# Turning the output in 32x32 squares on VectorE instead of transposing it on TensorE, in a spectral filter followed by a SiLU block

## Chip, cores, metric

One core of one Trainium2 chip. The metric is device time of one execution in microseconds; "before" has a median of 2844.55 us (2841.62 to 2846.77, 4 runs). In the text, TensorE is also PE, VectorE is DVE, ScalarE is ACT, GpSimd is POOL and SyncE is SP, as in the profile.

## The reference

```python
x: (8, 3008, 256) f32; filt_r, filt_i: (1505, 256) f32; w_in: (256, 2048); w_out: (2048, 256)
X = np.fft.rfft(x, axis=1)
y = np.fft.irfft(X * (filt_r + 1j * filt_i)[None], n=3008, axis=1).astype(np.float32)
h = y.reshape(24064, 256) @ w_in
out = (h / (1 + np.exp(-h)) @ w_out).astype(np.float32)
```

## The kernel before

The FFT is done as matmuls in three stages per batch (`spectral`: stage 1, forward, filter multiply, inverse, stage 3). Stage 3 leaves y with channels on the partitions and positions along the free dimension. A "half" of a batch has 16 x 94 = 1504 positions; three "pairs" of chunks cut them. Both products with the weights are done in 2x2 blocks with seven instead of eight block products (the w_t of sums and differences), over 8 steps per pair: in a step, `hidden` makes one slice of the hidden layer in the PSUM tiles px and pyz (one buffer each), and `project` multiplies the previous slice with w_out into `acc`. After the eighth step `drain` copies `acc` to s, seven adds combine it, and `output` transposes and stores. Pieces of the next batch's `spectral` are put between the rounds of these steps.

```python
PAIRS = [(0, 252), (504, 250), (1004, 250)]      # first position, columns of one chunk
CH = 252
...
        def stage3(u):
            g, cb = divmod(u, 2)
            if cb == 0 and g < 7:
                load_t4(g + 1)
            ps = bank(b, f"pd_{b}_{u}").rearrange("p a c -> p (a c)")
            psv = ps[:, 0:4 * NR].rearrange("p (a r) -> p a r", r=NR)      # NR = 94
            for i in range(4):
                nc.tensor.matmul(out=psv[:, i, :], lhsT=t4s[g][:, i, cb * 128:cb * 128 + 128],
                                 rhs=wi_t, start=True, stop=True)
            ...   # 376 columns, cut at the pairs' borders, evicted as they come: order n', row
                    evac(y[pair][:, cb, p0 - c0:p1 - c0], ps[:, p0 - lo:p1 - lo])
...
    def output(pair, chunk):
        b, half, c0, n = pairs[pair]
        s, m = results[pair], n // 2
        ps = fps.tile([128, 2, 2, 128], FP32, name=f"pt_{pair}_{chunk}", tag="f")
        for blk in range(2):
            for h in range(2):
                src = ((2, 6), (4, 1))[chunk][h]
                nc.tensor.transpose(out=ps[0:m, blk, h], in_=s[:, src, m * blk:m * blk + m],
                                    identity=id_t)
        o = opool.tile([128, 2, C], FP32, name=f"o_{pair}_{chunk}", tag="o")
        evac(o[0:m], ps[0:m].rearrange("p k h c -> p k (h c)"))     # DVE and ACT in turn
        for blk in range(2):
            store(o, blk, m, b, half, c0 + n * chunk + m * blk)     # rows of 1 KB, issued by POOL
...
        for g, (step, rnd) in enumerate(((-11, 3), (-7, 3), (-3, 3), (0, 3), (9, 3), (15, 6), (29, 3), (33, 3))):
            put(step, rnd, stage3, 2 * g); put(step, rnd, stage3, 2 * g + 1)
```

Of the kernel before, what the change touches and what calls it, by code (L numbers as in the profile page):

```python
# [49 lines left out]
NJP = NJ // 2  # L53
HALF = 16 * NR

PAIRS = [(0, 252), (504, 250), (1004, 250)]
CH = 252
STEPS = 2 * len(PAIRS) * NJP
LAG = 1

# [77 lines left out]
def kernel(  # L138
# [14 lines left out]
    wi_dram = nc.inline_tensor(wi_host, name="wi_tbl")  # L153
    d_dram = nc.inline_tensor(d_host, name="d_tbl")
    e_dram = nc.inline_tensor(e_host, name="e_tbl")
    id_dram = nc.inline_tensor(np.eye(128, dtype=np.float32), name="id_tbl")

    def pool(name, bufs, space=None):
        kw = {} if space is None else {"space": space}
        return ctx.enter_context(tc.tile_pool(name=name, bufs=bufs, **kw))  # L160

    cpool = pool("consts", 1)
    ypool = pool("y", 4)
    typool = pool("ty", 2)
    xpool = pool("x", 1)
    upool = pool("u", 1)
    t1pool = pool("t1", 2)
    t2pool = pool("t2", 2)
    ppool = pool("p", 2)
    zpool = pool("z", 3)  # L170
    qpool = pool("q", 2)
# [15 lines left out]
    f_t = [cpool.tile([128, NG, 2, C], FP32, name=f"filt{i}") for i in range(2)]  # L187

    w_t = cpool.tile([128, 7, 2, NJP, 128], FP32)
    id_t = cpool.tile([128, 128], FP32)  # L190
    warm = cpool.tile([128, 1], FP32)
    x_t = [xpool.tile([128, 2, 2, C], FP32, name=f"x{i}") for i in range(2)]

# [34 lines left out]
    def spectral(b):  # L228
# [7 lines left out]
        def load_x(u):  # L236

            if b == 0 and u < 4:
                xs[u] = ypool.tile([128, 2, 512], FP32, name=f"x_{b}_{u}", tag="y")
                nc.gpsimd.memset(xs[u][32:64], 0.0)  # L240
            else:
                xs[u] = x_t[u % 2]
            for h in range(2):
                for r0, nr in ((0, 32), (32, N1 - 32)):
                    nc.sync.dma_start(
                        out=xs[u][64 * h + r0:64 * h + r0 + nr],
                        in_=bass.AP(tensor=x.tensor,
                                    offset=x.offset + (b * S + 32 * r0 + 4 * u + 2 * h) * C,
                                    ap=[[32 * C, nr], [32 * N1 * C, 2], [1, 2 * C]]))
# [9 lines left out]

        def stage1(u):  # L260
            ut = us.pop(u)
            t1 = t1pool.tile([128, 2, 2, C], FP32, name=f"t1_{b}_{u}", tag="t1")
            ps = [bank(b, f"pa_{b}_{u}_{h}") for h in range(2)]
            for par in range(2):
                for h in range(2):
                    rows = slice(64 * h, 64 * h + N1)
                    nc.tensor.matmul(out=ps[h][64 * par:64 * par + 64], lhsT=wf_t[rows, par],  # L267
                                     rhs=ut[rows, par], start=True, stop=True)
            for h in range(2):
                evac(t1[:, h], ps[h])  # L270
            for par in range(2):
                nc.gpsimd.dma_start(  # L272
                    out=d1[par].rearrange("s p n c -> (s p) n c")[:, 4 * u:4 * u + 4, :],
                    in_=t1[64 * par:64 * par + 2 * NS].rearrange("p h n c -> p (h n) c"))

        def load_t2(g):
            t2s[g] = t2pool.tile([128, 4, C], FP32, name=f"t2_{b}_{g}", tag="t2")
            for par in range(2):
                nc.sync.dma_start(out=t2s[g][64 * par:64 * par + 64],
                                  in_=d1[par, 4 * g:4 * g + 4].rearrange("s p n c -> (p n) s c"))  # L280
# [52 lines left out]
        def stage3(u):  # L333
            g, cb = divmod(u, 2)
            half = g // 4
# [3 lines that stand above are left out]
            psv = ps[:, 0:4 * NR].rearrange("p (a r) -> p a r", r=NR)  # L339
            for i in range(4):  # L340
                nc.tensor.matmul(out=psv[:, i, :], lhsT=t4s[g][:, i, cb * 128:cb * 128 + 128],  # L341
                                 rhs=wi_t, start=True, stop=True)

            lo, hi = 4 * NR * (g % 4), 4 * NR * (g % 4 + 1)
            for k, (c0, n) in enumerate(PAIRS):
                p0, p1 = max(lo, c0), min(hi, c0 + 2 * n)
                if p0 < p1:
                    pair = (2 * b + half) * len(PAIRS) + k
                    if pair not in y:
                        y[pair] = ypool.tile([128, 2, 512], FP32, name=f"y_{pair}", tag="y")  # L350
                    evac(y[pair][:, cb, p0 - c0:p1 - c0], ps[:, p0 - lo:p1 - lo])

        at = STEPS * b
        pieces = []
# [15 lines left out]
            put(3 * g - 35, 1, add, g, 1)  # L370
            put(3 * g - 35, 3, inverse, g)
        put(-18, 5, load_t4, 0)
        for g, (step, rnd) in enumerate(((-11, 3), (-7, 3), (-3, 3), (0, 3), (9, 3), (15, 6), (29, 3), (33, 3))):
            put(step, rnd, stage3, 2 * g)
            put(step, rnd, stage3, 2 * g + 1)
        if b > 0:
# [9 lines left out]
    def combine(eng, out, in0, in1, op):  # L386
        eng.tensor_tensor(out=out, in0=in0, in1=in1, op=op)  # L387

    def tokens(pair):

        n, yt = pairs[pair][3], y[pair]
        t = typool.tile([128, 4, CH], FP32, name=f"ty_{pair}", tag="ty")
        combine(v, t[:, 0:2, 0:n], yt[:, :, n:2 * n],
                yt[:, 0, 0:2 * n].rearrange("p (a n) -> p a n", a=2), ALU.subtract)
        combine(v, t[:, 2, 0:n], yt[:, 1, n:2 * n], t[:, 0, 0:n], ALU.subtract)
        combine(v, t[:, 3, 0:n], yt[:, 1, 0:n], t[:, 2, 0:n], ALU.subtract)
        ty[pair] = t

    def hidden(step):

        pair, jp = divmod(step, NJP)
        n, yt, t = pairs[pair][3], y[pair], ty[pair]
        px = xps.tile([128, 512], FP32, name=f"px_{step}", tag="x")
        pyz = xps.tile([128, 2, 256], FP32, name=f"pyz_{step}", tag="yz")
        sums = abcpool.tile([128, 3, CH], FP32, name=f"abc_{step}", tag="abc")
# [70 lines left out]
    def drain(pair, i):  # L476
        n = pairs[pair][3]

        if i == 0:
            results[pair] = spool.tile([128, 8, CH], FP32, name=f"s_{pair}", tag="s")  # L480
        s = results[pair]
        copy = v.tensor_copy if i % 2 else nc.scalar.copy
        if i < 3:
            copy(out=s[:, 2 * i:2 * i + 2, 0:n], in_=acc[pair][i][:, :, 0:n])  # L484
            return
        copy(out=s[:, 6, 0:n], in_=acc.pop(pair)[3][:, 0, 0:n])
        eng = v if pair == len(pairs) - 1 else gp
        for o, a, b in ((2, 0, 2), (5, 0, 5), (3, 5, 3), (6, 3, 6), (0, 5, 1), (4, 0, 4), (1, 3, 1)):
            combine(eng, s[:, o, 0:n], s[:, a, 0:n], s[:, b, 0:n], ALU.add)

    def output(pair, chunk):

        b, half, c0, n = pairs[pair]
        s, m = results[pair], n // 2
        ps = fps.tile([128, 2, 2, 128], FP32, name=f"pt_{pair}_{chunk}", tag="f")
        for blk in range(2):
            for h in range(2):
                src = ((2, 6), (4, 1))[chunk][h]
                nc.tensor.transpose(out=ps[0:m, blk, h], in_=s[:, src, m * blk:m * blk + m],  # L499
                                    identity=id_t)  # L500
        o = opool.tile([128, 2, C], FP32, name=f"o_{pair}_{chunk}", tag="o")
        evac(o[0:m], ps[0:m].rearrange("p k h c -> p k (h c)"))
        for blk in range(2):
            store(o, blk, m, b, half, c0 + n * chunk + m * blk)

    def store(o, blk, m, b, half, col):
        p = 0
        while p < m:
            n, r = divmod(col + p, NR)
            cnt = min(m - p, NR - r)  # L510
            t0 = b * S + 32 * r + 16 * half + n
            nc.gpsimd.dma_start(  # L512
                out=bass.AP(tensor=out.tensor, offset=out.offset + t0 * C, ap=[[32 * C, cnt], [1, C]]),
                in_=o[p:p + cnt, blk, :])
            p += cnt

    wide = moe_w_in.dtype != FP32
    nc.vector.memset(warm, 0.0)
# [7 lines left out]
    def places(j, w):  # L526
        first, by = PLACES[j % 2][w]
        return w_t[:, first:first + by + 1:by, w, j // 2]

    def load_weights(j):  # L530

# [7 lines left out]
    def round_weights(j):  # L539
# [15 lines left out]
        v.scalar_tensor_tensor(out=mf, in0=lo, scalar=2.0 ** -52, in1=mf, op0=ALU.mult, op1=ALU.add)  # L555
        for w in range(2):
            cols = slice(256 * w, 256 * w + 256)
            gp.tensor_tensor(out=places(j, w), in0=mf[:, cols].rearrange("p (k n) -> p k n", k=2),
                             in1=ef[:, cols].rearrange("p (k n) -> p k n", k=2), op=ALU.mult)
        if j % 2:  # L560
            combine_weights(j // 2)
        if j + 2 < NJ:
# [2 lines left out]
    def load_exact(j):  # L565
        for k in range(2):
            nc.sync.dma_start(out=places(j, 0)[:, k],
                              in_=moe_w_in[128 * k:128 * k + 128, 128 * j:128 * j + 128])
            nc.sync.dma_start(out=places(j, 1)[:, k],
                              in_=moe_w_out[128 * j:128 * j + 128, 128 * k:128 * k + 128])  # L570
        if j % 2:
            combine_weights(j // 2)

# [8 lines left out]
    def constants():  # L582
# [1 line left out]
        load_filters()  # L584
        nc.scalar.dma_start(out=e_t, in_=e_dram.ap())
        nc.scalar.dma_start(out=wi_t, in_=wi_dram.ap())
        nc.scalar.dma_start(out=id_t, in_=id_dram.ap())

    nc.sync.dma_start(out=wf_t, in_=wf_dram.ap())
    for xt in x_t:  # L590
# [15 lines left out]
        pending += [(-39 + 1.9 * j, NJ, lambda j=j: load_exact(j)) for j in range(NJ)]  # L606
    per = len(PAIRS) * 2

    stores = ((10, 3), (18, 6), (30, 3), (35, 3), (43, 3), (51, 6))
    for pair in range(len(pairs)):  # L610
        pending.append((NJP * pair - 2 + (5 if pair % per == 3 else 1) / ROUNDS, 100,
                        lambda pair=pair: tokens(pair)))
        step, rnd = stores[pair % per]
        for chunk in range(2):
            pending.append((pair // per * STEPS + step + rnd / ROUNDS, 99 + chunk,
                            lambda pair=pair, chunk=chunk: output(pair, chunk)))
    pending.sort(key=lambda p: p[:2])
# [49 lines left out]
```

## Time and profile before

| | before |
|---|---|
| span of the profiled run | 2842.5 us |
| PE / DVE / ACT / POOL busy | 2713 / 1627 / 1103 / 726 us |
| one batch in mid-kernel | 336.27 us, PE idle 1.5 us of it |
| the 8 transposes of a pair, in PE's stream | 0.88 us |
| transposes' evictions | 96, of 0.69 us (DVE) or 0.59 us (ACT) |
| stores | 432, issued by POOL, 0.53 us each |

"Busy" is time in which an engine has an instruction in flight. PE's instructions overlap, so their summed durations exceed their cost; the cost of a PE group is read from the starts in the timeline. PEld is TensorE loading the weights of a matmul; an "eviction" is the copy of a finished PSUM tile to SBUF by DVE or ACT; the "granted clock" is the share of full speed that TensorE was given. In the timeline, a row has start, length, engine, line, operation, out<-in, shape and count; what stands in brackets is the engine's idle time just before and what ended it.

### The profile page before, as it was taken

What the parts mean: (1) busy time and instruction counts of PE and PEld (TensorE: products, weight loads), DVE (VectorE), ACT (ScalarE), POOL (GpSimd) and SP (SyncE); (2) the same over time, 40 slices, a digit from 0 to 9 for tenths busy, and PEclk for the clock granted to TensorE, in tenths of its full rate; (3) what the DMA queues carried; (4) which work ended last, traced back from release to release, by engine and by line L of the source; (5) the groups of instructions that cost most, each with busy time, mean ns of one, the idle gap of its engine ahead of it and who ended that gap; (6) DMA issues with size and microseconds to landing.
All of it is one profiled execution on the core that took longest, in us unless ns stands there. A gap on an engine that the chain in (4) does not pass through costs nothing.

```text
span 2842.5 us, 39974 instructions
## 1 busy us (share of the span) xinstructions
PE 2713.2 (95%) x14976; PEld 2292.8 (81%) x14976; DVE 1627.1 (57%) x3416; ACT 1103.0 (39%) x3058; POOL 725.9 (26%) x1155
## 2 busy tenths in 40 slices
PE   2479999999999999999999999999999999999998
PEld 0258889788897888888898888978888788988887
DVE  2876654666556665566655665465655666544554
ACT  0124334443444334443344443444344433444443
POOL 1532222222213312222222232223221321221222
PEclk9779999999999999999999999999999999999999
DMA  8543211232113211232112321123111321000000
GB/s 177 157 120 84 60 34 37 80 74 51 34 35 105 60 42 31 52 98 64 36 36 70 84 50 34 43 79 77 43 39 33 105 63 42 27 28 18 14 15 15
DMA packets 92276, 166.66 MB, mean 59 GB/s; under 512 B 20641, under 2 KB 51441, under 8 KB 91825
## 3 DMA queue, kind: packets, MB, share of 16 engines
q1 hardware_dynamic: 56080, 83.46, 11.2%
q0 software_dynamic: 33536, 75.03, 10.2%
q10 hardware_dynamic: 2464, 5.61, 1.1%
q8 instruction: 118, 1.93, 0.3%
q14 instruction: 78, 0.63, 0.1%
HBM read 89.03 MB, written 74.97 MB: 58 GB/s over the span
## 4 chain that ended last, share of the span: by engine, by line
PE 92%; DVE 4%; DMA 2%; issue 1%; POOL 1%; ACT 0%; SPq 0%; DVEq 0%; ACTq 0%; POOLq 0%
PE acc L468 39%; PE px L412 23%; PE pyz L412 17%; PE pd L341 4%; PE pc L319 3%; PE pa L267 2%; PE pb L290 2%; PE pt L499 1%; DMA filt<-in_filt_r_dram 1%; DVE z L310 0%; DMA d<-t 0%; DVE u L255 0%; DVE g L387 0%; DVE z L309 0%; DMA t<-d 0%
## 5 line engine op out<-in xcount | busy, mean ns | idle before, releaser
L468 PE MATMUL acc<-g,w_t 128*128 128x250 f32 (+1 forms) x5376 | 1512.1, 375 | 0.4 <-DVE g L387 0.4
L468 PEld LDWEIGHTS acc<-g,w_t 128*128 128x128 f32 x5376 | 1021.1, 190 | 116.0 <-DVE g L387 0.8
L387 DVE TENSOR_TENSOR g<-pyz,abc 128x250 f32<-128x250 f32 (+1 forms) x1152 | 480.2, 417 | 641.9 <-ACT abc L433 363.2
L387 DVE TENSOR_TENSOR g<-g 128x250 f32<-128x250 f32 (+3 forms) x1152 | 611.7, 531 | 197.1 <-ACT g L416 183.7
L412 PE MATMUL px<-ty,w_t 128*128 128x250 f32 (+1 forms) x2304 | 692.9, 382 | 0.5 <-ACT abc L433 0.5
L416 ACT ACTIVATE g<-g 128x250 f32<-128x250 f32 (+1 forms) x1152 | 474.0, 411 | 241.2 <-DVE g L387 241.2
L412 PEld LDWEIGHTS px<-ty,w_t 128*128 128x128 f32 x2304 | 415.1, 190 | 123.0 <-issue 71.6
L412 PE MATMUL pyz<-y,w_t 128*128 128x250 f32 (+1 forms) x1536 | 452.8, 376 | 8.8 <-DVE g L387 8.8
L387 POOL TENSOR_TENSOR s<-s 128x250 f32<-128x250 f32 (+1 forms) x329 | 266.4, 826 | 678.3 <-DVE s L484 428.8
L512 POOL DMA_DIRECT2D out_dram<-o x432 | 223.7, 526 | 502.5 <-DVE o L211 495.0
L412 PEld LDWEIGHTS pyz<-y,w_t 128*128 128x128 f32 x1536 | 282.7, 189 | 52.5 <-DVE g L387 15.4
L427 ACT COPY abc<-px 128x250 f32<-128x250 f32 (+1 forms) x384 | 141.7, 369 | 379.7 <-PE px L412 379.7
L416 ACT ACTIVATE g<-px 128x250 f32<-128x250 f32 (+1 forms) x384 | 146.4, 381 | 298.4 <-PE px L412 298.4
L326 POOL DMA_DIRECT2D d<-q x192 | 113.8, 601 | 555.7 <-DVE q L211 553.0
L433 ACT COPY abc<-px 128x250 f32<-128x250 f32 (+1 forms) x384 | 142.0, 370 | 228.0 <-PE px L412 228.0
L412 PE MATMUL pyz<-ty,w_t 128*128 128x250 f32 (+1 forms) x768 | 225.8, 376 | 0.0
L412 PE MATMUL px<-y,w_t 128*128 128x250 f32 (+1 forms) x768 | 225.2, 375 | 0.0
L412 PEld LDWEIGHTS pyz<-ty,w_t 128*128 128x128 f32 x768 | 145.5, 190 | 17.6 <-DVE g L387 1.4
L412 PEld LDWEIGHTS px<-y,w_t 128*128 128x128 f32 x768 | 143.5, 189 | 19.2 <-issue 0.4
L272 POOL DMA_DIRECT2D d<-t x128 | 65.9, 519 | 344.3 <-ACT abc L433 275.9
L341 PEld LDWEIGHTS pd<-wi_t,t 96*128 96x128 f32 x1024 | 129.3, 199 | 20.6 <-issue 11.7
L341 PE MATMUL pd<-wi_t,t 96*128 96x94 f32 x1024 | 128.1, 280 | 17.0 <-issue 11.0
(46 smaller groups left out, 1504.2 us busy)
## 6 DMA issues: line engine op xcount, KB each, us to landing
d<-t POOLq DMA_DIRECT2D x128, 192.0 KB, 3.0
t<-d SPq DMA_DIRECT2D x96, 256.0 KB, 4.0
d<-q POOLq DMA_DIRECT2D x192, 128.0 KB, 2.7
t<-d SPq DMA_DIRECT2D x64, 384.0 KB, 3.8
x<-in_x_dram SPq DMA_DIRECT2D x128, 128.0 KB, 3.1
x<-in_x_dram SPq DMA_DIRECT2D x128, 60.0 KB, 2.9
out_dram<-o POOLq DMA_DIRECT2D x80, 94.0 KB, 2.0
raw<-in_moe_w_in_dram SPq DMA_DIRECT2D x16, 256.0 KB, 2.8
```

The costliest lines, as they stand in the source:

```text
L267: nc.tensor.matmul(out=ps[h][64 * par:64 * par + 64], lhsT=wf_t[rows, par], rhs=ut[rows, par], start=True, stop=True)
L272: nc.gpsimd.dma_start(out=d1[par].rearrange("s p n c -> (s p) n c")[:, 4 * u:4 * u + 4, :], in_=t1[64 * par:64 * par + 2 * NS].rearrange(" ...
L319: nc.tensor.matmul(out=ps[i][:, k, :], lhsT=e_t[rows, g, k, ri, :], rhs=zs[k][rows, ri, :], start=(ri == 0), stop=(ri == 1))
L326: nc.gpsimd.dma_start(out=d2[a0:a0 + 2, :, :].rearrange("s n c -> n s c"), in_=qt[64 * p:64 * p + 64, :, :])
L341: nc.tensor.matmul(out=psv[:, i, :], lhsT=t4s[g][:, i, cb * 128:cb * 128 + 128], rhs=wi_t, start=True, stop=True)
L387: eng.tensor_tensor(out=out, in0=in0, in1=in1, op=op)
L412: nc.tensor.matmul(out=out, lhsT=w_t[:, c, 0, jp], rhs=rhs, start=start, stop=True, skip_group_check=True)
L416: nc.scalar.activation(out=g[:, k, 0:n], in_=g[:, k, 0:n] if src is None else src, func=AFT.Silu)
L427: nc.scalar.copy(out=sums[:, 1, 0:n], in_=xo)
L433: nc.scalar.copy(out=sums[:, 2, 0:n], in_=xo)
L468: nc.tensor.matmul(out=acc[pair][i][:, h, 0:n], lhsT=w_t[:, c, 1, jp], rhs=g[:, k, 0:n], start=(jp == 0 and h == 0), stop=last, skip_group ...
L512: nc.gpsimd.dma_start(out=bass.AP(tensor=out.tensor, offset=out.offset + t0 * C, ap=[[32 * C, cnt], [1, C]]), in_=o[p:p + cnt, blk, :])
```

## The change

The intent is to take the transposes off TensorE. VectorE can transpose 32x32 squares from SBUF to SBUF. For squares to become runs of the output, w_out's columns are permuted as they are loaded, and the tokens are taken in the order row, n' (so y is now one tile for a whole half and stage 3 must be complete before a half's first tokens). Stores go to SP, in runs of 256 bytes. Chunks are multiples of 16.

```diff
-PAIRS = [(0, 252), (504, 250), (1004, 250)]
-CH = 252
+PAIRS = [(0, 256), (512, 256), (1024, 240)]
+CH = 256
...
-            lo, hi = 4 * NR * (g % 4), 4 * NR * (g % 4 + 1)
-            ... (evictions cut at the pairs' borders)
+            if cb == 0 and g % 4 == 0:
+                y[b, half] = ypool.tile([128, 2, HALF], FP32, name=f"y_{b}_{half}", tag="y")
+            evac(y[b, half][:, cb].rearrange("p (r n) -> p n r", n=16)[:, 4 * (g % 4):4 * (g % 4) + 4],
+                 psv)
...
-        for g, (step, rnd) in enumerate(((-11, 3), (-7, 3), (-3, 3), (0, 3), (9, 3), (15, 6), (29, 3), (33, 3))):
+        for g, (step, rnd) in enumerate(((-16, 3), (-12, 3), (-8, 3), (-4, 3), (9, 3), (12, 6), (15, 6), (18, 6))):
...
     def output(pair, chunk):
-        ... (four nc.tensor.transpose, one evac, stores issued by POOL)
+        o = opool.tile([128, 8, 2, 32], FP32, name=f"o_{pair}_{chunk}", tag="o")
+        for h in range(2):
+            v.transpose(out=o[:, :, h, :], in_=results[pair][:, ((2, 6), (4, 1))[chunk][h], :])
+        row = (c0 + n * chunk) // 16
+        for rr in range(2):
+            cnt = (n // 16 - rr + 1) // 2
+            t0 = b * S + 32 * (row + rr) + 16 * half
+            for q in range(4):
+                p0 = 32 * q + 16 * rr
+                nc.sync.dma_start(out=bass.AP(..., ap=[[C, 16], [64 * C, cnt], [1, 64]]),
+                    in_=o[p0:p0 + 16, 0:cnt].rearrange("p k h c -> p k (h c)"))
... (also: permuted loading of w_out, t1 and t2 in one pool of two buffers, y pool of two halves,
     a memset of the unused columns of s, other steps for the outputs, no identity table)
```

More of the change, by code (lines that the diff above doesn't have):

```diff
@@ L155 @@
     e_dram = nc.inline_tensor(e_host, name="e_tbl")
-    id_dram = nc.inline_tensor(np.eye(128, dtype=np.float32), name="id_tbl")
     def pool(name, bufs, space=None):
@@ L162 @@
     cpool = pool("consts", 1)
-    ypool = pool("y", 4)
+    ypool = pool("y", 2)
     typool = pool("ty", 2)
@@ L166 @@
     upool = pool("u", 1)
-    t1pool = pool("t1", 2)
-    t2pool = pool("t2", 2)
+    tpool = pool("t12", 2)
     ppool = pool("p", 2)
@@ L189 @@
     w_t = cpool.tile([128, 7, 2, NJP, 128], FP32)
-    id_t = cpool.tile([128, 128], FP32)
     warm = cpool.tile([128, 1], FP32)
@@ L238, in load_x @@
             if b == 0 and u < 4:
-                xs[u] = ypool.tile([128, 2, 512], FP32, name=f"x_{b}_{u}", tag="y")
+                if u % 2 == 0:
+                    xs[u, "y"] = ypool.tile([128, 2, HALF], FP32, name=f"x_{b}_{u}", tag="y")
+                xs[u] = xs[u - u % 2, "y"][:, u % 2, 0:1024].rearrange("p (a n) -> p a n", a=2)
                 nc.gpsimd.memset(xs[u][32:64], 0.0)
@@ L261, in stage1 @@
             ut = us.pop(u)
-            t1 = t1pool.tile([128, 2, 2, C], FP32, name=f"t1_{b}_{u}", tag="t1")
+            t1 = tpool.tile([128, 2, 2, C], FP32, name=f"t1_{b}_{u}", tag="t")
             ps = [bank(b, f"pa_{b}_{u}_{h}") for h in range(2)]
@@ L276, in load_t2 @@
         def load_t2(g):
-            t2s[g] = t2pool.tile([128, 4, C], FP32, name=f"t2_{b}_{g}", tag="t2")
+            t2s[g] = tpool.tile([128, 4, C], FP32, name=f"t2_{b}_{g}", tag="t")
             for par in range(2):
@@ L342, in stage3 @@
                                  rhs=wi_t, start=True, stop=True)
-            lo, hi = 4 * NR * (g % 4), 4 * NR * (g % 4 + 1)
-            for k, (c0, n) in enumerate(PAIRS):
-                p0, p1 = max(lo, c0), min(hi, c0 + 2 * n)
-                if p0 < p1:
-                    pair = (2 * b + half) * len(PAIRS) + k
-                    if pair not in y:
-                        y[pair] = ypool.tile([128, 2, 512], FP32, name=f"y_{pair}", tag="y")
-                    evac(y[pair][:, cb, p0 - c0:p1 - c0], ps[:, p0 - lo:p1 - lo])
+            if cb == 0 and g % 4 == 0:
+                y[b, half] = ypool.tile([128, 2, HALF], FP32, name=f"y_{b}_{half}", tag="y")
+            evac(y[b, half][:, cb].rearrange("p (r n) -> p n r", n=16)[:, 4 * (g % 4):4 * (g % 4) + 4],
+                 psv)
         at = STEPS * b
@@ L387, in combine, with channels @@
         eng.tensor_tensor(out=out, in0=in0, in1=in1, op=op)
+    def channels(pair):
+        b, half, c0, n = pairs[pair]
+        return y[b, half][:, :, c0:c0 + 2 * n]
     def tokens(pair):
-        n, yt = pairs[pair][3], y[pair]
+        n, yt = pairs[pair][3], channels(pair)
         t = typool.tile([128, 4, CH], FP32, name=f"ty_{pair}", tag="ty")
@@ L401, in hidden @@
         pair, jp = divmod(step, NJP)
-        n, yt, t = pairs[pair][3], y[pair], ty[pair]
+        n, yt, t = pairs[pair][3], channels(pair), ty[pair]
         px = xps.tile([128, 512], FP32, name=f"px_{step}", tag="x")
@@ L480, in drain @@
             results[pair] = spool.tile([128, 8, CH], FP32, name=f"s_{pair}", tag="s")
+            if n < CH:
+                gp.memset(results[pair][:, :, n:CH], 0.0)
         s = results[pair]
@@ L493, in output @@
         b, half, c0, n = pairs[pair]
-        s, m = results[pair], n // 2
-        ps = fps.tile([128, 2, 2, 128], FP32, name=f"pt_{pair}_{chunk}", tag="f")
-        for blk in range(2):
-            for h in range(2):
-                src = ((2, 6), (4, 1))[chunk][h]
-                nc.tensor.transpose(out=ps[0:m, blk, h], in_=s[:, src, m * blk:m * blk + m],
-                                    identity=id_t)
-        o = opool.tile([128, 2, C], FP32, name=f"o_{pair}_{chunk}", tag="o")
-        evac(o[0:m], ps[0:m].rearrange("p k h c -> p k (h c)"))
-        for blk in range(2):
-            store(o, blk, m, b, half, c0 + n * chunk + m * blk)
-    def store(o, blk, m, b, half, col):
-        p = 0
-        while p < m:
-            n, r = divmod(col + p, NR)
-            cnt = min(m - p, NR - r)
-            t0 = b * S + 32 * r + 16 * half + n
-            nc.gpsimd.dma_start(
-                out=bass.AP(tensor=out.tensor, offset=out.offset + t0 * C, ap=[[32 * C, cnt], [1, C]]),
-                in_=o[p:p + cnt, blk, :])
-            p += cnt
+        o = opool.tile([128, 8, 2, 32], FP32, name=f"o_{pair}_{chunk}", tag="o")
[7 more added lines that the diff above has]
+                p0 = 32 * q + 16 * rr
+                nc.sync.dma_start(
+                    out=bass.AP(tensor=out.tensor, offset=out.offset + t0 * C + 64 * q,
+                                ap=[[C, 16], [64 * C, cnt], [1, 64]]),
+                    in_=o[p0:p0 + 16, 0:cnt].rearrange("p k h c -> p k (h c)"))
     wide = moe_w_in.dtype != FP32
@@ L528, in places, with columns @@
         return w_t[:, first:first + by + 1:by, w, j // 2]
+    def columns(ap, w):
+        if w == 0:
+            return ap.rearrange("p (k n) -> p k n", k=2)
+        return ap.rearrange("p (q k i) -> p k q i", q=4, k=2)
     def load_weights(j):
@@ L557, in round_weights @@
             cols = slice(256 * w, 256 * w + 256)
-            gp.tensor_tensor(out=places(j, w), in0=mf[:, cols].rearrange("p (k n) -> p k n", k=2),
-                             in1=ef[:, cols].rearrange("p (k n) -> p k n", k=2), op=ALU.mult)
+            dst = places(j, w) if w == 0 else places(j, w).rearrange("p k (q i) -> p k q i", q=4)
+            gp.tensor_tensor(out=dst, in0=columns(mf[:, cols], w), in1=columns(ef[:, cols], w),
+                             op=ALU.mult)
         if j % 2:
@@ L568, in load_exact @@
                               in_=moe_w_in[128 * k:128 * k + 128, 128 * j:128 * j + 128])
-            nc.sync.dma_start(out=places(j, 1)[:, k],
-                              in_=moe_w_out[128 * j:128 * j + 128, 128 * k:128 * k + 128])
+            nc.sync.dma_start(out=places(j, 1)[:, k].rearrange("p (q i) -> p q i", q=4),
+                              in_=columns(moe_w_out[128 * j:128 * j + 128, :], 1)[:, k])
         if j % 2:
@@ L586, in constants @@
         nc.scalar.dma_start(out=wi_t, in_=wi_dram.ap())
-        nc.scalar.dma_start(out=id_t, in_=id_dram.ap())
     nc.sync.dma_start(out=wf_t, in_=wf_dram.ap())
@@ L607 @@
     per = len(PAIRS) * 2
-    stores = ((10, 3), (18, 6), (30, 3), (35, 3), (43, 3), (51, 6))
+    stores = (((10, 1), (10, 5)), ((19, 5), (20, 1)), ((28, 5), (29, 1)), ((34, 1), (34, 5)),
+              ((42, 1), (42, 5)), ((50, 1), (51, 1)))
     for pair in range(len(pairs)):
@@ L612 @@
                         lambda pair=pair: tokens(pair)))
-        step, rnd = stores[pair % per]
         for chunk in range(2):
+            step, rnd = stores[pair % per][chunk]
             pending.append((pair // per * STEPS + step + rnd / ROUNDS, 99 + chunk,
```

## The prediction

> **What bounds the kernel now.** I read the page first (engine shares, the rows by slice, the chain that ended last), then the busy time by stretch, the waits, the groups by shape and the timeline. The page of the kernel before:
>
> ```profile
> span 2842.5 us, 39974 instructions
> PE 2713.2 (95%) x14976; PEld 2292.8 (81%) x14976; DVE 1627.1 (57%) x3416; ACT 1103.0 (39%) x3058; POOL 725.9 (26%) x1155
> ...
> PE   2479999999999999999999999999999999999998
> ...
> PE 92%; DVE 4%; DMA 2%; issue 1%; POOL 1%; ACT 0%; SPq 0%; DVEq 0%; ACTq 0%; POOLq 0%
> ```
>
> TensorE is busy in nine tenths of every slice but the first three and the last, and 92% of the chain is its work. "Busy" alone proves little, since matmuls overlap, so I took one whole period in mid-kernel from the view of busy time by stretch:
>
> ```profile
> 1190.47:1526.74 336.27, 334.72 (x1874) 284.37 (x1873) 195.72 (x415) 136.40 (x382) 84.58 (x136) 1.00 0.22 57
> ```
>
> One batch takes 336.27 us; PE is idle 1.55 us of it, at a granted clock of 1.00. DVE (195.72) and ACT (136.40) have large gaps, and the DMA engines are 22% busy. PE's waits over the whole run confirm it: the sizeable ones belong to the start, and the one steady wait is small.
>
> ```profile
> PE pa L267 <- DVE u L255: 48.0, 8, 28.6
> ...
> PE pc L319 <- DVE z L309: 33.6, 7, 7.7
> ...
> PE pyz L412 <- DVE g L387: 8.8, 13, 0.9
> ```
>
> So in the steady stage the time is the sum of what PE streams: a matmul removed is time saved, and one removed from another engine is worth nothing by itself.
>
> **What the Trainium skill says.** (1) "TensorE: Matmul & The Clock Gate", Part 4: a PE transpose takes any 128x128 in one shot, but lands in PSUM and needs a copy after it; about 275 ns in a kernel. The trace agrees (273 ns and a copy of 586 or 692 ns), yet 273 ns is a duration, not the price: the timeline shows what it costs in the stream. (2) "VectorE: DVE Perf Modes", The three transpose paths: VectorE transposes 32x32 blocks only, into SBUF, 311 ns for 128x128 bf16. No transpose on DVE is in this trace; I price it below from this trace's copies. (3) "DMA: Bandwidth & Descriptors", Specifications: line rate needs transfers of at least 512 B. The new runs of 256 B fall below; the trace doesn't yet show such stores. (4) "SBUF — State Buffer", the note on 16-byte cachelines: accesses that change line each time pay. The new evictions into y step 64 B; the ones before are contiguous, so the trace is silent on it.
>
> **The change, part by part.**
>
> PE, removed. Each of 48 pairs had 8 transposes. Around them the stream looks so:
>
> ```profile
> 1260.98 0.58 PE L468 MATMUL acc<-g,w_t 128*128 128x250 f32 x2
> 1261.40 1.04 PE L499 MATMUL pt<-id_t,s 128*126 128x128 f32 x8
> 1262.28 0.59 PE L412 MATMUL px<-ty,w_t 128*128 128x250 f32 x2
> ```
>
> From 1261.40 to the next start at 1262.28 is 0.88 us, so 0.11 us each; the other pairs that I looked at have 0.87 to 0.88 too. 47 pairs lie inside the stream: 47 x 0.88 = 41.4 us. (The chain's 1.4% for this line, 40 us, says the same. The 50 us of summed durations overstates it.)
>
> PE, resized. A product is recorded as two MATMULs; two start 0.42 us apart at 250 columns (1260.98 to 1261.40), 0.211 us each. With 0.110 us for 128 columns the slope is 0.101 / 122 = 0.83 ns a column, with a floor of some 4 ns. Before, a half has 252 + 250 + 250 = 752 columns; after, 256 + 256 + 240 = 752. The number of matmuls stays, so the sum stays: 0 us. At 240 columns a matmul needs about 0.203 us, still over the 0.190 us of a weight load, so no new limit. Forward, inverse and stage 3 matmuls are the same.
>
> DVE and ACT. Out go 96 evictions of the transposes, half on DVE (0.69 us) and half on ACT (0.59):
>
> ```profile
> L499 PE MATMUL pt<-id_t,s 128*125 128x128 f32 x256 | 33.9, 274 | 2.0 <-DVE s L387 2.0
> L211 DVE COPY o<-pt 125x512 f32<-125x512 f32 x32 | 22.1, 690 | 17.0 <-PE pt L499 16.3
> L213 ACT COPY o<-pt 125x512 f32<-125x512 f32 x32 | 18.8, 586 | 36.2 <-PE pt L499 36.2
> L486 DVE COPY s<-acc 128x250 f32<-128x250 f32 x32 | 13.2, 413 | 4.1 <-PE acc L468 4.0
> ```
>
> In come 48 x 2 x 2 = 192 DVE transposes of 128x256. DVE copies take 413 ns at 250 columns and about 691 at 512: 1.06 ns a column, so an estimated 0.42 us each, 81 us in all. DVE gains 81 - 48 x 0.69 = 48 us, ACT loses 28. The evictions into y fall from 192 to 128 instructions but write with a 64 B step; were each twice as long, DVE's half would gain another 35 us. DVE then stands near 60%: no bound. What can reach PE is latency: an output puts two transposes (0.84 us) and perhaps some semaphore waits into DVE's queue, ahead of the adds that free the single px/pyz buffers. One copy of 0.69 us does the same today, and PE's steady DVE waits total 8.8 us. There will be 96 such places instead of 48; I charge 3 us.
>
> POOL and DMA. 432 issues by POOL (223.7 us) go; its seven adds after each drain stay, at 0.83 us each. 768 stores move to SP, whose issues take 0.31 to 0.60 us in this trace: an estimated 350 us, spread over the run. The output's packets grow from 24,064 of 1 KB to 96,256 of 256 B. In the trace 376 B packets take 22 ns and 1 KB ones of the store queue 49; even at 50 ns for each short one the addition is 96,256 x 50 / 16 = 0.30 ms per engine less 0.07 ms, some 8% of the span on engines now about 23% busy. Hidden.
>
> The start. Now all four stage 3 groups of a half must be done before its first tokens, as these are ordered by row. For batch 0 the fourth moves ahead of the first step (it ran at 180.04 us, after the first products at 176.34). DVE is the busy one there (72 of the 87 us from 100 to 187), rounding weights, and that work stays. The added chain is one load of about 4 us, partly under the last roundings, against 1.8 us of PE work that no longer falls inside step 0. I charge +1 us, give or take 4.
>
> The end. After the last product DVE drains and adds, then come transposes, a copy and 9 POOL issues:
>
> ```profile
> 2830.90 2.76 DVE L387 TENSOR_TENSOR s<-s 128x250 f32<-128x250 f32 x7
> ...
> 2833.48 0.83 PE L499 MATMUL pt<-id_t,s 128*125 128x128 f32 x4 [0.28 <-DVE s L387]
> ...
> 2834.55 4.64 POOL L512 DMA_DIRECT2D out_dram<-o x9 [28.57 <-DVE o L211]
> ```
>
> After the change: adds end near 2833.7, the first two transposes 0.84 us later, then 16 issues of SP at about 0.45 us (7.2), then some 2 us to land: 2843.7 against 2842.5, +1 us.
>
> Sum: 2844 - 41.4 + 3 + 1 + 1 = 2807.6; as the three charges are cautious, I say 2806 us, 1.3% less.
>
> **The rivals.** *DVE becomes the wait.* If a transpose took 1 us or more, or the strided evictions doubled and came just before an add that PE needs, each of 96 outputs and 128 evictions could stall PE by some 0.1 to 0.3 us: 10 to 40 us, which eats the gain (2815 to 2845). For it: px and pyz have one buffer each. Against it: DVE is idle 42% of the period, and today's 0.69 us copies leave PE waiting 1.4 us a batch. *SP becomes the wait.* The stores stand in the queue that brings x, t2 and t4, and a store waits there for its transposes; 8 issues are 3.6 us. For it: in-order queue, four times the packets. Against it: loads are issued 1.6 steps or more (over 10 us) ahead and take 3 to 4. If it failed in each batch, +5 us x 8: 2845. *POOL's relief helps.* The adds after a drain no longer queue behind issues and DVE meets fewer port conflicts; but PE waits for neither, so at most a few us (2800). *The prologue moves.* Before 187 us PE loses over 100 us to waits, so a reordering there could give or take 5 to 10 us whatever the transposes do.
>
> **Range and chances.** The 41 us is read from a stream with 0.5% of idle time; the doubts are the start (+-4), the end (+-2) and DVE's latency (0 to 12, one-sided). That gives 2796 to 2819. Faster by over 2% needs 2788, 15 us beyond what PE can give: 0.03. Slower by over 2% needs a new wait of 100 us: 0.02. Within 2%: 0.95.
>
> **What would show it.** Right: no PE transposes, 14,592 matmuls, a batch period of 336.27 - 6 x 0.88 = 331.0 us with PE idle below 3 us, DVE transposes near 0.42 us, DVE near 59%, POOL's busy time down by 220 us. Wrong: PE waits on DVE g or on a t<-d load in mid-kernel, transposes of 0.8 us and more, a first full step later than 187 us, or an end more than 5 us longer after the last product.

## The result, and the profile after

The changed kernel takes 2808.59 us (2807.75 to 2809.27, 4 runs) against 2844.55: a ratio of 0.9874, 95% interval 0.9857 to 0.9891. Here and below, a ratio is the mean time of one kernel's fast runs over that of the other's fast runs of the same rounds, so it is not quite the ratio of the medians quoted.

The page of the changed kernel (its first lines, and the DMA line below the slices):

```profile
span 2806.0 us, 39589 instructions
## 1 busy us (share of the span) xinstructions
PE 2671.0 (95%) x14592; PEld 2255.6 (80%) x14592; DVE 1671.9 (60%) x3528; ACT 1089.1 (39%) x2978; POOL 504.5 (18%) x739
...
DMA packets 184546, 166.56 MB, mean 59 GB/s; under 512 B 121120, under 2 KB 151456, under 8 KB 184096
```

PE has lost 384 instructions, all of them transposes. DVE gained 45 us, POOL lost 221, and short packets went up sixfold. The bound is the same as before. Busy time by stretch, one batch in mid-kernel (columns: stretch, its length, then busy time and count for PE, PEld, DVE, ACT and POOL, granted clock, DMA share, GB/s):

```profile
961.92:1293.16 331.24, 329.70 (x1827) 279.71 (x1826) 201.38 (x429) 134.67 (x370) 56.77 (x84) 1.00 0.24 58
```

A batch takes 331.24 us instead of 336.27: 5.03 us less, with PE idle for the same 1.5 us. The groups by shape, for the operations that are new or altered:

```profile
L497 DVE STREAM_TRANSPOSE o<-s 128x256 f32<-128x256 f32 x192 | 73.7, 422 | 0.3 <-issue 0.3
...
L211 ACT COPY y<-pd 128x376 f32<-128x376 f32 x64 | 51.1, 799 | 123.4 <-PE pd L341 123.4
L209 DVE COPY y<-pd 128x376 f32<-128x376 f32 x64 | 51.0, 797 | 86.1 <-PE pd L341 86.1
```

and the same eviction of 376 columns in the kernel before:

```profile
L211 DVE COPY y<-pd 128x376 f32<-128x376 f32 x32 | 17.6, 550 | 39.1 <-PE pd L341 39.1
...
L213 ACT COPY y<-pd 128x376 f32<-128x376 f32 x32 | 15.1, 472 | 63.7 <-PE pd L341 63.7
```

A VectorE transpose takes 422 ns. The evictions into y, which now write one element every 64 bytes, went from 550 and 472 ns to about 800 on either engine. The waits over the whole run (who waited for whom, total, times, longest; then the same view of SP's own queue):

```profile
PE pyz L411 <- DVE g L382: 8.5, 12, 1.0
```

```profile
SPq L504 <- DVE o L497: 1255.3, 54, 54.6
```

PE's one steady wait for DVE was 8.8 us before and is 8.5 now. SP's queue stands 1255 us at stores, waiting for their transposes; that looks alarming and, as PE's waits show, holds nothing up.

To see where the 36.5 us between the two spans lie, I cut each run at two events of the timeline: the first stage 1 matmuls that fall between products (batch 1's), and the end of the last product. The first rows are of before, the second of after:

```profile
187.74 1.09 PE L267 MATMUL pa<-u,wf_t 47*64 47x512 f32 x8
...
2828.58 1.95 PE L468 MATMUL acc<-g,w_t 128*128 128x250 f32 x8 [0.41 <-DVE g L387]
```

```profile
189.67 1.09 PE L267 MATMUL pa<-u,wf_t 47*64 47x512 f32 x8
...
2790.37 1.89 PE L467 MATMUL acc<-g,w_t 128*128 128x240 f32 x8 [0.41 <-DVE g L382]
```

So the "start" grew from 187.7 to 189.7, the "stream" between the events shrank from 2642.8 to 2602.6, and the "tail" after the last product grew from 12.0 to 13.7: +1.9 - 40.2 + 1.8 = -36.5 us.

### The profile page after: what moved, and what is told of

It is laid out like the page before. It is cut to its first block, busy times and chain, and to the rows that moved or that the text cites. A ratio compares the mean times of both kernels' runs of the same rounds, so it can differ in the third digit from the quotient of the medians.

```text
span 2806.0 us, 39589 instructions
## 1 busy us (share of the span) xinstructions
PE 2671.0 (95%) x14592; PEld 2255.6 (80%) x14592; DVE 1671.9 (60%) x3528; ACT 1089.1 (39%) x2978; POOL 504.5 (18%) x739
## 4 chain that ended last, share of the span: by engine, by line
PE 92%; DVE 4%; DMA 2%; issue 1%; POOL 0%; ACT 0%; SPq 0%; DVEq 0%; ACTq 0%; POOLq 0%
PE acc L467 40%; PE px L411 24%; PE pyz L411 17%; PE pd L341 4%; PE pc L319 3%; PE pa L267 2%; PE pb L290 2%; DVE g L382 1%; DMA x<-in_x_dram 1%; DVE u L255 1%; DVE z L310 0%; DMA d<-t 0%; DVE z L309 0%; DMA t<-d 0%; DMA filt<-in_filt_i_dram 0%
## 5 line engine op out<-in xcount | busy, mean ns | idle before, releaser
L467 PE MATMUL acc<-g,w_t 128*128 128x256 f32 (+1 forms) x5376 | 1512.6, 375 | 0.4 <-DVE g L382 0.4
L382 DVE TENSOR_TENSOR g<-pyz,abc 128x256 f32<-128x256 f32 (+1 forms) x1152 | 479.7, 416 | 614.8 <-ACT abc L432 356.8
L382 DVE TENSOR_TENSOR g<-g 128x256 f32<-128x256 f32 (+3 forms) x1152 | 611.0, 530 | 196.6 <-ACT g L415 183.5
L411 PE MATMUL px<-ty,w_t 128*128 128x256 f32 (+1 forms) x2304 | 694.3, 383 | 0.5 <-ACT abc L432 0.5
L415 ACT ACTIVATE g<-g 128x256 f32<-128x256 f32 (+1 forms) x1152 | 473.0, 411 | 238.4 <-DVE g L382 235.9
L411 PE MATMUL pyz<-y,w_t 128*128 128x256 f32 (+1 forms) x1536 | 454.0, 377 | 8.5 <-DVE g L382 8.5
L382 POOL TENSOR_TENSOR s<-s 128x256 f32<-128x256 f32 (+1 forms) x329 | 265.7, 825 | 1040.4 <-DVE s L485 520.1
L426 ACT COPY abc<-px 128x256 f32<-128x256 f32 (+1 forms) x384 | 141.4, 368 | 381.0 <-PE px L411 381.0
L432 ACT COPY abc<-px 128x256 f32<-128x256 f32 (+1 forms) x384 | 142.7, 372 | 285.0 <-PE px L411 284.8
L411 PE MATMUL pyz<-ty,w_t 128*128 128x256 f32 (+1 forms) x768 | 226.4, 377 | 0.0
L411 PE MATMUL px<-y,w_t 128*128 128x256 f32 (+1 forms) x768 | 225.7, 376 | 0.0
L419 ACT COPY abc<-px 128x256 f32<-128x256 f32 (+1 forms) x384 | 134.1, 349 | 0.1
## 6 DMA issues: line engine op xcount, KB each, us to landing
d<-t POOLq DMA_DIRECT2D x128, 192.0 KB, 3.0
```

The costliest lines, as they stand in the source:

```text
L382: eng.tensor_tensor(out=out, in0=in0, in1=in1, op=op)
L411: nc.tensor.matmul(out=out, lhsT=w_t[:, c, 0, jp], rhs=rhs, start=start, stop=True, skip_group_check=True)
L415: nc.scalar.activation(out=g[:, k, 0:n], in_=g[:, k, 0:n] if src is None else src, func=AFT.Silu)
L419: nc.scalar.copy(out=sums[:, 0, 0:n], in_=xo)
L426: nc.scalar.copy(out=sums[:, 1, 0:n], in_=xo)
L432: nc.scalar.copy(out=sums[:, 2, 0:n], in_=xo)
```

## The experiments

My theory: the gain is the PE time of the transposes and nothing else, less small losses at the start, at the end and in the stream. The rivals: the new chunk sizes, the relief of POOL and of the PSUM buffers, or a cost of the vector work that hides a larger gain. All runs below are right except e5, which is wrong on purpose. Each was timed beside runs of the kernel before (median 2844.1 to 2845.4 us). The start of one and the same prologue varies: over the nine profiles of kernels that share the changed kernel's start (but for its evictions) it lies between 189.1 and 192.7 us. The stream does not vary so: where nothing in it was altered it is 2602.6 or 2602.7 us, four times out of four.

| run | median us | ratio to before | start | stream | tail |
|---|---|---|---|---|---|
| before | 2844.55 | 1 | 187.7 | 2642.8 | 12.0 |
| after | 2808.59 | 0.9874 | 189.7 | 2602.6 | 13.7 |
| e1 sizes alone | 2845.73 | 1.0001 | 188.8 | 2643.3 | 11.9 |
| e2 PE transposes back | 2850.48 | 1.0021 | 189.1 | 2644.7 | 13.7 |
| e3 DVE transposes twice | 2811.65 | 0.9886 | 191.3 | 2604.4 | 14.4 |
| e4 DVE transposes four times | 2895.56 | 1.0180 | 191.7 | 2688.8 | 15.7 |
| e5 plain evictions | 2806.14 | 0.9865 | 190.2 | 2600.6 | 13.7 |
| e6 stores from POOL | 2813.43 | 0.9892 | 192.4 | 2603.2 | 17.4 |
| e7 shorter end | 2805.40 | 0.9864 | 192.7 | 2602.6 | 9.3 |
| e8 earlier loads at the start | 2805.80 | 0.9866 | 188.6 | 2602.7 | 13.7 |
| e9 = e7 + e8 | 2802.51 | 0.9848 | 190.9 | 2602.6 | 9.4 |
| e10 evictions in runs of four | 2806.26 | 0.9862 | 192.0 | 2600.6 | 13.7 |
| e11 the same, by PE's order | 2805.76 | 0.9859 | 189.5 | 2601.1 | 13.7 |
| e12 = e7 + e8 + e11 | 2800.45 | 0.9844 | 189.3 | 2600.7 | 9.4 |

### e1: the sizes alone

```diff
 (kernel before)
-PAIRS = [(0, 252), (504, 250), (1004, 250)]
-CH = 252
+PAIRS = [(0, 256), (512, 256), (1024, 240)]
+CH = 256
```

> The kernel before with pairs of 256, 256 and 240 columns in place of 252, 250 and 250, and nothing else; right results. Theory (TensorE's stream sets the time, 0.83 ns a column plus a floor per matmul): 752 columns a half either way, so the same within 2 us of 2844. Rival (part of the gain comes from sizes that suit the engines better): 10 to 36 us less. If 256 were worse by itself: more than 2850.

Measured: ratio 1.0001 (0.9988 to 1.0013), stream 0.5 us longer. The sizes bring nothing by themselves; they are there because squares of 32 and runs of 16 need them. The sum of columns is the same, and so is the time.

### e2: the TensorE transposes put back

```diff
 (changed kernel, in output)
+        ps = fps.tile([128, 2, 2, 128], FP32, name=f"pt_{pair}_{chunk}", tag="f")
+        for blk in range(2):
+            for h in range(2):
+                nc.tensor.transpose(out=ps[:, blk, h], identity=id_t,
+                                    in_=results[pair][:, ((2, 6), (4, 1))[chunk][h], 128 * blk:128 * blk + 128])
... (also: the identity table and its load)
```

> The changed kernel with the eight TensorE transposes of each pair put back beside the vector engine's, into a PSUM buffer that nobody reads; right results. Theory (the gain is TensorE's removed work, 0.88 us a pair, 48 pairs): 40 to 43 us over the changed kernel, about 2850. Rival (the gain came from the copies, the PSUM buffers or POOL's 432 issues): 0 to 15 us more, under 2825.

Measured: 41.9 us over the changed kernel, by the medians. All of it is in the stream: 2644.7 - 2602.6 = 42.1 us. The groups by shape show the transposes at the duration that they had before:

```profile
L503 PE MATMUL pt<-id_t,s 128*128 128x128 f32 x384 | 58.0, 273 | 2.0 <-DVE s L384 2.0
```

This kernel has everything else of the change: no eviction of transposes, no issue of stores by POOL, DVE transposes, SP stores. It is 0.2% slower than the kernel before. So the removed PE work is the whole gain, and the rest of the change costs about 1.9 us in the stream (2644.7 to 2642.8), 0.5 us of which e1 has too.

### e3 and e4: how much vector work stays hidden

```diff
 (changed kernel, in output)
-        for h in range(2):
+        for h in [0, 1] * 2:        # e4: * 4
             v.transpose(out=o[:, :, h, :], in_=results[pair][:, ((2, 6), (4, 1))[chunk][h], :])
```

> The changed kernel with each of the vector engine's transposes issued twice (same source and target); right results. It adds 192 x 0.42 = 81 us of vector work, in 96 lumps of 0.84 us. Theory (the vector engine is idle 40% of the period and its queue has slack): up to 8 us more. Rival (its latency decides the adds that TensorE waits for): 30 to 80 us more.

> As the run with doubled transposes, but four times: 96 lumps of 3.4 us of vector work where the change has 0.84. Theory: now longer than the slack between an add and the matmul that needs its buffer (about 1 us by the waits), so 96 x 1 to 2.5 us: 80 to 240 us more, which shows where hidden ends. Rival (vector work stays hidden as long as the engine has idle time in total): under 20 us more.

A "lump" is the vector work that one `output` puts into DVE's queue at once. In the timeline (changed kernel, e3, e4):

```profile
991.49 0.77 DVE L497 STREAM_TRANSPOSE o<-s 128x256 f32<-128x256 f32 x2
```

```profile
994.24 1.42 DVE L497 STREAM_TRANSPOSE o<-s 128x256 f32<-128x256 f32 x4
```

```profile
1014.02 2.73 DVE L497 STREAM_TRANSPOSE o<-s 128x256 f32<-128x256 f32 x8
```

Transposes in a row overlap: one lasts 0.42 us, but the next starts some 0.33 us after it. The lumps are therefore 0.77, 1.42 and 2.73 us and not 0.84, 1.7 and 3.4, as the expectations had it from summed durations, and the transposes keep DVE busy for 73.7, 136.3 and 261.3 us.

Measured: doubled, 63 us more of vector work lengthen the stream by 1.8 us. Fourfold, 188 us more lengthen it by 86.2 us. There are 94 lumps in the stream (47 pairs, two chunks), so e4 loses 0.92 us a lump on average. The waits of PE in e4:

```profile
PE pyz L411 <- DVE g L382: 70.3, 88, 1.4
```

DVE still has idle time in total: it is busy 64% of e4's span. What ran out is the distance between an add that empties the single pyz buffer and the matmul that needs it: a lump may grow from 0.77 to 1.42 us for nearly nothing, and at 2.73 us it is paid for. Where between the two the payment begins no run shows; if each further microsecond cost a full one, it would be at 2.73 - 0.92 = 1.8 us (an estimate). So the change's own lumps are hidden, with room.

### e5, e10, e11: the strided evictions

```diff
 (changed kernel, in stage3; e5, wrong order on purpose)
-            evac(y[b, half][:, cb].rearrange("p (r n) -> p n r", n=16)[:, 4 * (g % 4):4 * (g % 4) + 4],
-                 psv)
+            evac(y[b, half][:, cb, 376 * (g % 4):376 * (g % 4) + 376], ps[:, 0:376])
 (e10: the same elements in the order row, n)
+            evac(y[b, half][:, cb].rearrange("p (r n) -> p r n", n=16)[:, :, 4 * (g % 4):4 * (g % 4) + 4],
+                 psv.rearrange("p a r -> p r a"))
 (e11: psv is made with "p (r a) -> p a r", a=4, so that PE writes columns 16 bytes apart; eviction
  as e10, from ps[:, 0:4 * NR] in its own order)
```

> The changed kernel with the evictions of stage 3 written contiguously (376 columns as they come, no step of 64 bytes); the tokens are then in a wrong order and the result is wrong on purpose. Theory: an eviction falls from 0.80 us to 0.55 (vector) and 0.47 (scalar engine), and that is hidden, except for the four of batch 0 at the start: 0 to 3 us less. Rival (the strided evictions hold the PSUM buffers and cost TensorE time in every batch): 5 us or more less.

> The changed kernel with the evictions of stage 3 in the order row, then n: each writes runs of four neighbouring elements (16 bytes) every 64 bytes, and reads PSUM with a step of 376 bytes instead; right results. Theory (the write that leaves its 16-byte line each time is what makes 0.55 and 0.47 us into 0.80): evictions back at 0.45 to 0.6 us and 1 to 3 us less in all, as with the contiguous ones. Rival (a strided PSUM read costs the same, or the step of 64 bytes counts whatever the run): still about 0.8 us, and no gain.

> As the run with runs of four, but TensorE writes its columns into PSUM 16 bytes apart, so that the eviction reads PSUM contiguously and writes runs of four; right results. Theory: evictions 0.45 to 0.6 us. If a strided PSUM write slows the matmuls (512 of stage 3, recorded as 1024): their mean rises over 283 ns and the stream by up to 1024 x 0.05 = 50 us; rival (TensorE doesn't mind): 1 to 3 us less than the changed kernel.

Measured: with contiguous evictions (e5) the stream is 2.0 us shorter, about as much as e2 left open. e10 gets the same 2.0 us with a right result. Its groups by shape:

```profile
L209 DVE COPY y<-pd 128x376 f32<-128x376 f32 x64 | 35.1, 549 | 86.5 <-PE pd L341 86.5
L211 ACT COPY y<-pd 128x376 f32<-128x376 f32 x64 | 30.2, 472 | 124.2 <-PE pd L341 124.2
```

Runs of four elements, 16 bytes, bring the evictions from 800 ns back to the 549 and 472 ns of contiguous ones, although PSUM is now read with a step of 376 bytes. This is what the Trainium skill's note on 16-byte cachelines ("SBUF — State Buffer") leads one to expect of the write side: the cost is in leaving the line at each element, not in the step. e11 moves the step to PE's writes and is as good (evictions 549 and 472 ns, stage 3 matmuls at 283 ns as in the changed kernel, stream 2601.1; that is 0.5 us more than in e10, and its weight loads for pyz wait 30 times for DVE instead of 28).

Why the stream feels an eviction of 0.8 us shows in the waits of PE's weight loads (before, then the changed kernel):

```profile
PEld px L412 <- ACT abc L433: 2.5, 15, 0.2
```

```profile
PEld px L411 <- ACT abc L432: 6.7, 36, 0.2
```

In e5, e10 and e11 this wait is gone from the stream. One of the 36 places in the changed kernel:

```profile
1076.31 0.80 ACT L211 COPY y<-pd 128x376 f32<-128x376 f32 x1 [1.12 <-PE pd L341]
1076.91 0.41 ACT L432 COPY abc<-px 128x256 f32<-128x256 f32 x1
...
1077.37 0.30 PEld L411 LDWEIGHTS px<-ty,w_t 128*128 128x128 f32 x2 [0.17 <-ACT abc L432]
```

ACT's eviction of y stands before the copy that frees the single px buffer, so the copy comes late and px's next weight load waits 0.17 us for it. At the same place in e10 the eviction takes 0.47 us and nothing waits. Laid side by side, the matmuls of the two traces start at the same distances (to 0.02 us) except at 36 places, all of this kind, where the changed kernel loses 0.056 us each: the 2.0 us. DVE's slower evictions cost nothing that the traces show. As the kernel before has 15 such waits itself, the 2.0 us are not quite the 1.9 us that e2 left open.

### e6: the stores issued by POOL

```diff
-                nc.sync.dma_start(
+                nc.gpsimd.dma_start(
```

> The changed kernel with the stores issued by POOL, as before, in place of SP; right results. Theory (which queue issues is hidden in mid-kernel): within 3 us, with the end later by 16 x (0.55 - 0.45), up to 3 us. Rival (SP's queue delays loads, so POOL is better): 3 us or more less. Rival (POOL's relief was part of the gain): 5 us or more more.

Measured: 4.8 us over the changed kernel, more than expected, but not where either rival put it: the stream is 2603.2, 0.6 us longer. The tail is 3.7 us longer, and the start of the profiled run happened to be 2.7 us later, within what starts vary by. The tail in the timeline:

```profile
2799.60 8.44 POOL L504 DMA_DIRECT2D out_dram<-o x16 [29.29 <-DVE o L497]
```

The 16 issues take 8.4 us against SP's 7.5, and from the last issue to the end of the span it is 5.0 us against 2.5. In mid-kernel the choice between POOL and SP is worth 0.6 us in these profiles, and PE's waits differ there by a single one (for DVE at pyz: 8.9 us in 13 waits against 8.5 in 12). In neither run does PE wait there for a load.

### e7 and e8: the two ends

```diff
 (e7: the last pair alone)
...          # (the seven adds, counted by k)
             combine(eng, s[:, o, 0:n], s[:, a, 0:n], s[:, b, 0:n], ALU.add)
+            if eng is v and k == 3:
+                output(pair, 0)
+        if eng is v:
+            output(pair, 1)
...
+                eng = nc.scalar if pair == len(pairs) - 1 and q % 2 else nc.sync
... (also: the last pair's outputs are no longer put in by step)
 (e8: batch 0 alone: groups 2 and 3 are loaded behind stage 3 of groups 0 and 1)
-            if cb == 0 and g < 7:
+            if cb == 0 and g < 7 and (b > 0 or g == 0 or g >= 4):
                 load_t4(g + 1)
...
+            if cb == 1 and b == 0 and g < 3:
+                load_t4(g + 2)
```

> The changed kernel with the last pair's end shortened: chunk 0 is transposed and stored after the fourth of the seven adds, and half of the last 16 stores are issued by ACT beside SP; right results. In the trace those 16 issues take 7.5 us after the transposes. Theory: they set the end, so 3.5 to 5 us less. Rival (what ends last is the landing of the bytes): under 1 us less.

> The changed kernel with, for batch 0 alone, the stage 3 loads of groups 2 and 3 issued two groups ahead, so that they no longer stand behind the last weight loads; right results. Theory (the first products start at 179.1 us because group 2's load lands at 172.2): first products 3 to 4 us earlier, the whole 2 to 4 us less. Rival (the vector engine's rounding of weights decides the start): under 1 us less.

In the changed kernel the end looks so (adds, transposes, issues):

```profile
2792.62 2.68 DVE L382 TENSOR_TENSOR s<-s 128x240 f32<-128x240 f32 x7
2795.22 1.42 DVE L497 STREAM_TRANSPOSE o<-s 128x256 f32<-128x256 f32 x4
2796.01 7.51 SPq L504 DMA_DIRECT2D out_dram<-o x16
```

and in e7, on two queues:

```profile
2798.03 3.74 SPq L509 DMA_DIRECT2D out_dram<-o x8
2798.04 3.94 ACTq L509 DMA_DIRECT2D out_dram<-o x8
```

The tail falls from 13.7 to 9.3 us, 4.4 us, inside the expected range: the issuing of 16 small stores was what ended last. From the last product to the first issue it is 2.75 us instead of 3.75 (the earlier chunk); the other 3.5 us or so are the second queue. By the medians e7 gained 3.2 us, a little under the range.

The start of the changed kernel, and of e8 (PE's timeline):

```profile
172.19 7.11 PE L341 MATMUL pd<-wi_t,t 96*128 96x94 f32 x32 [4.99 <-DMA t<-d]
179.10 1.11 PE L411 MATMUL px<-y,w_t 128*128 128x256 f32 x2
```

```profile
171.65 3.70 PE L341 MATMUL pd<-wi_t,t 96*128 96x94 f32 x16 [0.51 <-DMA t<-d]
175.22 1.19 PE L413 MATMUL px<-y,w_t 128*128 128x256 f32 x2
178.40 1.19 PE L413 MATMUL px<-ty,w_t 128*128 128x256 f32 x2 [0.93 <-DVE ty L384]
```

The wait of 5 us for group 2's load is gone and the first product starts 3.9 us earlier, as expected. But PE then waits for the tokens that DVE makes and, at the same place, its weight load waits 1.63 us for weights that POOL combines; and it runs on at half its clock. Busy time by stretch in e8 (the first figure after the counts is the granted clock):

```profile
175.00:186.50 11.50, 10.10 (x23) 6.16 (x23) 5.98 (x10) 3.71 (x9) 3.67 (x5) 0.52 0.32 81
187.00:200.00 13.00, 13.00 (x67) 9.50 (x66) 7.90 (x17) 5.32 (x14) 2.09 (x4) 1.00 0.28 74
```

In the first stretch the granted clock is 0.52, and rows of products that wait for nothing start 0.86 us apart (183.05 to 183.91); after some 186 us it is 1.00, and they start 0.43 us apart (186.34 to 186.77). In the changed kernel the stretch from 179 to 186.5 us, with its own first products, has 0.66 already. By batch 1's first stage 1 matmuls only 1.1 us are left, less than starts vary by. The medians say 2.8 us less; a gain of one to three microseconds is likely and not shown beyond doubt.

### e9 and e12: a version that beats both

> The changed kernel with both the shortened end and the earlier loads of batch 0; right results. Theory: the two parts are apart in time and add up: 5 to 7 us less than the changed kernel, about 2802. Rival (they share a limit): 3 us less.

> The changed kernel with the shortened end, the earlier loads of batch 0, and evictions in runs of four with TensorE's columns 16 bytes apart in PSUM; right results. Theory: the three gains of the runs alone add up: the stream as in the run with runs of four (2 us shorter), the end 4.4 us shorter, the start about 2 us earlier; 7 to 9 us less than the changed kernel, about 2800. Rival: no further gain over the run with start and end (2802.5).

e9 has 2802.51 us, 6.1 us less than the changed kernel where e7 and e8 had 3.2 and 2.8: the two parts add up, within the noise. e12 adds the evictions of e11 and has 2800.45 us (2798.1 to 2801.13, 5 runs), a ratio of 0.9844 to the kernel before; it is 8.1 us faster than the changed kernel by the medians and right. Its stream and tail are those of the parts alone (2600.7 and 9.4).

## Why the prediction was right, step by step

- **PE is the bound, and 8 transposes cost 0.88 us a pair: 41.4 us.** Right. Putting them back (e2) costs 42.1 us in the stream. The page's 50 us of summed durations would have been too much, as said.
- **The sizes cost and bring nothing.** Right (e1: 1.0001).
- **A DVE transpose takes 0.42 us, priced from copies of this trace; DVE rises to about 60%.** Right: 422 ns, 60%. But the 0.84 us for two and the 81 us in all are sums of durations; two in a row take 0.77 us, and all of them 73.7 us.
- **3 us for latency on DVE.** The size was near (2 us) by luck, for the cause was another. The prediction charged it to the 96 lumps of transposes; e3 shows that even a second lump of the same size costs only 1.8 us in all, and e5 and e10 that 2.0 us come from the evictions with a step of 64 bytes, by way of ACT and px. The prediction has those as work for DVE that might double, and in a rival as a possible stall of DVE's adds, but put no part of its 3 us on them and did not look at ACT, whose evictions grew the more (1.7 times, against 1.45 on DVE).
- **The expected batch period of 331.0 us.** 331.24. In e10, without those waits, it is 330.95 (1184.25 to 1515.20).
- **POOL and DMA are hidden.** Right in effect (e6). The packets before were misread: the trace has only 272 of 1,024 bytes on POOL's queue and carried nearly all the output in packets of 2 to 4 KB, so there were not 24,064 of 1 KB. And the price of a 256 byte store was set far too high: at most 50 ns was assumed, 19.9 ns is the mean in the trace. The DMA engines rose from 22% to 24% of a batch instead of by 8 points.
- **Start +1 us, give or take 4.** +1.9 in the two profiles; the mean of the nine starts of this prologue, 190.9, against the two of the old one (187.7 and 188.8) makes it 2.7. The working let the added load lie partly under the last roundings. It stood behind the weight loads in SP's queue instead (e8).
- **End +1 us.** +1.8. The 7.2 us for 16 issues were 7.5, the 2 us to land 2.5.
- **Rivals.** DVE as the wait, SP as the wait and a gain from POOL's relief are all refuted by e3, e6 and the stream. The prologue did move, by 2 to 3 us, less than that rival's 5 to 10. The threat from DVE was real at four times the work (e4), not at one.
- **The sum.** 2807.6 by its parts, then lowered to 2806; measured 2808.6. That it is so close is in part luck: the stream gained 40.2 us where the parts said 38.4, and start and end cost 3.7 us where they said 2.

## What to carry to other kernels

Where one engine's stream has half a percent of idle time, price a removed piece by the distance between its neighbours' starts, and expect just that. Moving work to an engine that is 60% busy is free only while each lump stays shorter than the slack of the buffer that this engine empties; doubling and quadrupling the new work on purpose brackets that slack in two runs. Look at the waits of the weight loads too: waits of at most 0.2 us there, which PE's own list does not show, were the whole 2.0 us of the strided evictions. When a layout change turns a write into single elements far apart, keep at least 16 bytes together, and at the end of a kernel count the issues of small stores, not their bytes.

## What the Trainium skill lacked or had wrong

- "VectorE: DVE Perf Modes", The three transpose paths, has a time for 128x128 bf16 alone. A 128x256 fp32 transpose took 422 ns, like a copy from PSUM of the same width (425 ns in the changed kernel); in a row they start 0.33 us apart (eight in 2.73 us).
- "SBUF — State Buffer", the note on 16-byte cachelines, gives no size for the penalty on VectorE or ScalarE. Here 376 fp32 elements written 64 bytes apart took 797 ns (DVE) and 799 ns (ACT) against 549 and 472 in runs of four, so 16 bytes were enough. The same note says that any non-contiguous PSUM access slows matmuls significantly: e11's matmuls, writing 16 bytes apart, show the same 283 ns mean, and the stream didn't grow. At 94 columns these are spaced 0.11 us apart in both kernels, so some tens of ns could hide under their weight loads.
- "DMA: Bandwidth & Descriptors", Issuing engines are not separate DMA queues, says that issuing from several engines saves only the sequencer's time, usually small beside the DMA. At this kernel's end it was the larger part: 16 issues of SP took 7.5 us, where a store lands in 1.8, and a second queue took 4.4 us off the tail together with the earlier chunk.
- The same page, Specifications, asks for 512 B for line rate. Stores of 256 B took 19.9 ns a packet (12.9 bytes per ns and engine) against 48.6 ns for the 272 packets of 1 KB on POOL's queue before (21 bytes per ns) and 65.7 ns for SP's own loads in packets of 1 KB (15.6): slower per byte, as it says, and without effect here.
- None of the pages used here says how much slack a queue in program order has before an engine that reads a single PSUM buffer feels it; e3 and e4 put it between 1.42 and 2.73 us of lump in this kernel.
